# Recalibrating a build-time scheduler: the table of instruction durations is set to the pitches and latencies of a trace

## The chip, the core and the metric

The kernel runs on one NeuronCore of a Trainium2 chip. The metric is the device time of one execution in microseconds (us); lower is better. The engines are named as in the profile: PE (TensorE, matmuls; PEld is its weight load), ACT (ScalarE), DVE (VectorE), POOL (GpSimd), SP (SyncE, which issues the DMAs here).

## The reference

The kernel computes a transformer block with layer norms ahead of attention and of the feed-forward part, in bfloat16, for one sequence of 2048 tokens of width 1024, with 32 heads of 32 and a hidden width of 3584:

```python
def _A_ref(x, wqkv, wo):                       # attention
    qkv = (x @ wqkv).reshape(B, S, 3, H, Dh)   # H = 32, Dh = 32
    ...
    scores = jnp.einsum("bhqd,bhkd->bhqk", q, k) * scale
    p = _softmax(scores, axis=-1)
    o = jnp.einsum("bhqk,bhkd->bhqd", p, v)
    return o.transpose(...).reshape(B, S, D) @ wo

def _B_ref(x, w1, b1, w2, b2):                 # feed-forward
    h = _gelu(jnp.einsum("bsd,df->bsf", x, w1) + b1)   # tanh form
    return jnp.einsum("bsf,fd->bsd", h, w2) + b2

h  = x + _A_ref(_layernorm(x), A_wqkv, A_wo)
h2 = h + _B_ref(_layernorm(h), B_w1, B_b1, B_w2, B_b2)
```

## The kernel before

The program is a straight line of instructions for each engine, with no loop at run time. When it is built, Python code first describes the work as tasks in a graph (`Graph.add`): a task has an engine, one or several instructions, the buffers it reads and writes, a priority, an *occupancy* (`occ`, how long its engine is taken) and a *latency* (`lat`, how long after that its result can be used by another engine). `Graph.schedule` then plays the tasks through in time: whenever an engine is free by these figures, it takes one of the tasks whose inputs are ready by these figures. The order in which each engine takes its tasks in that play is the order in which its instructions are written into the program. `Graph.assign` adds the semaphore waits that the dependencies need. The figures themselves reach the chip in no other way: an instruction starts there when it is at the head of its engine's queue and its semaphores are there, whatever the plan thought.

The choice on ACT, DVE, POOL and SP is by priority and then by position in the list of tasks. PE has a rule of its own, `pick_pe`: a score matmul task (`qk`) goes first if it is ready; the value matmuls (`pv`) and the denominator matmuls (`den`) follow when enough rounds are waiting (`PV_FORCE = 3`, `PV_START = 6`); otherwise the next task of the background (`bg`) is taken, that is, projections, output projection, FFN and transposes. PE is in one of three tiling modes, `row` for qk (four matmuls of 32 rows at once), `col` for pv, den and narrow background (four of 32 columns at once), and `full`; a change of mode is charged `switch`. `merge_tiles` turns some runs of narrow background tasks back into full matmuls after the order is fixed.

The work is tiled as follows. There are 8 query blocks of 256 tokens (`qb`) and 8 head groups of 4 heads (`g`), so 64 attention jobs, each with 8 rounds (`r`) of 256 keys. One round is one qk task of eight matmuls (L769), two exponentials of 128x1024 from PSUM into SBUF on ACT (L779), a pv task of eight matmuls (L805), an addition of key halves on DVE (L820) and a denominator task against a matrix of ones (L834). Scores use PSUM banks 0 to 5 as three units of two banks, and a round takes two units, so that the qk of the next round needs the first exponential of this one to be done. Banks 6 and 7 are slots for attention results and for background.

In time there is a *lead* (x is loaded, normalised and transposed, keys and values of the first head group are projected half a chunk at a time, and two jobs of attention run beside it), then the other head groups and query blocks with the rest of the projections, late queries, the output projection (`wo`, evicted at L910), the second layer norm (`ln2`), `ffn1` (evicted at L943, with GELU by a tanh at L965 on ACT) and `ffn2` (evicted at L989) as background, and at the end the part of the last query block that needs the last attention results: `wo(7)`, `ln2(7)`, `ffn1(7)` (L540, GELU at L952) and `ffn2(7)`. Narrow background matmuls have line L534, their merged form L537, full ones L540; transposes by PE are L604, their evictions L611 and L613; L598 is the layer norm's scaling and L583 its statistics. Weights come through rings of buffers: 4 blocks of 512 KB for `wo` and `ffn1` (`a_w1r`) and 7 for `ffn2` (`a_w2r`).

Of the kernel before, what the change touches and what calls it, by code (L numbers as in the profile page):

```python
# [10 lines left out]
E = mybir.EngineType  # L11
# [49 lines left out]
class Graph:  # L61
# [44 lines left out]
        return t  # L106


    def schedule(self, pick_pe, pool, switch=0.1, dma_rate=280.0, dma_lat=2.1, dma_issue=0.06):
        for i, t in enumerate(self.tasks):  # L110
            t.left = len(t.deps)
            for d in t.deps:
# [8 lines left out]
        n = 0  # L121
# [207 lines left out]
def build_kernel(nc, A_x, A_wqkv, A_wo, B_w1, B_b1, B_w2, B_b2, out):  # L329
# [154 lines left out]
    B_qd = [[gr.buf() for _ in range(NCH)] for _ in range(G)]  # L484


    MM = 0.2195
    def c_dve_ps(n):
        return (120 + n) / 960.0 + 0.02

    def c_dve(n, x=1):
        return (62 + n / x) / 960.0 + 0.085

    def c_act(n, ap_bias=False):
        return 0.073 + (0.093 if ap_bias else 0.0) + n / 1200.0

    def pe(fns, occ, reads=(), writes=(), kind="bg", mode="full", prio=0, after=()):
        return gr.add(E.PE, fns, occ, 0.16, reads, writes, prio, kind, mode, after)

    def slot(nrel=1):  # L500
        return Slot(gr.buf(), nrel, (6, 7))
# [13 lines left out]
    def bb(bank):  # L515
        return bank.buf if isinstance(bank, Slot) else B_ps[bank]
# [10 lines left out]
    def mm(bank, lhsT, rhs, start, stop, reads, narrow, cols=(0, 512), after=()):  # L527

        c0, c1 = cols
        occ = MM * (c1 - c0) / 512.0 + 0.003  # L530
        if narrow:
            fns = []
            for j in range(4):
                fns.append(lambda p, j=j: p.matmul(psum[32 * j:32 * j + 32, bi(bank), c0:c1], lhsT[:, 32 * j:32 * j + 32], rhs,  # L534
                                                   start=start, stop=stop, tile_position=(0, 32 * j), skip_group_check=True))
            t = pe(fns, occ, reads=reads, writes=[bb(bank)], mode="col", after=after)
            t.whole = lambda p: p.matmul(psum[:, bi(bank), c0:c1], lhsT, rhs, start=start, stop=stop,  # L537
                                         skip_group_check=True)
        else:
            t = pe(lambda p: p.matmul(psum[:, bi(bank), c0:c1], lhsT, rhs, start=start, stop=stop),  # L540
                   occ, reads=reads, writes=[bb(bank)], mode="full", after=after)
        take(t, bank)

    def act(fn, n, reads=(), writes=(), prio=0, ap_bias=False, kind="", after=()):
        return gr.add(E.Activation, fn, c_act(n, ap_bias), 0.14, reads, writes, prio, kind, after=after)

    def dve(fn, occ, reads=(), writes=(), prio=0):
        return gr.add(E.DVE, fn, occ, 0.08, reads, writes, prio)

    def pool(fn, occ, reads=(), writes=(), prio=0):  # L550
        return gr.add(E.Pool, fn, occ, 0.1, reads, writes, prio)
# [22 lines left out]
    def layer_norm(tiles, prio, norm="dve", stats=None):  # L574

        n = len(tiles)
        while cnt["ln"] % NLN + n > NLN:
            cnt["ln"] += 1
        i = cnt["ln"] % NLN
        cnt["ln"] += n  # L580
        for k, (x_ap, B_x, o_ap, B_o) in enumerate(tiles):
            for c in range(2):
                dve(lambda v, c=c, k=k, x_ap=x_ap: v.bn_stats(st_l[:, i + k, 6 * c:6 * c + 6], x_ap[:, 512 * c:512 * c + 512]),  # L583
                    0.68, reads=B_x if isinstance(B_x, list) else [B_x], writes=[B_stl[i + k]], prio=(prio or 1) if stats is None else stats)
            dve(lambda v, k=k: v.bn_aggr(mv_l[:, i + k, :], st_l[:, i + k, :]), 0.2,  # L585
                reads=[B_stl[i + k]], writes=[B_mv[i + k]], prio=prio)
        sl = slice(i, i + n)
        pool(lambda g: g.tensor_copy(mvb[:, sl, :], mv_l[:, sl, :]), 0.25, reads=B_mv[sl], writes=B_mvb[sl], prio=prio)  # L588
        dve(lambda v: v.tensor_copy(mvr[:, sl, :], mvb[:, sl, 0:1]), 0.2, reads=B_mvb[sl], writes=B_mvr[sl], prio=prio)
        pool(lambda g: g.tensor_scalar(tb[:, sl, :], mvb[:, sl, 1:2], EPS_BF, None, ALU.add), 0.25,  # L590
             reads=B_mvb[sl], writes=B_tb[sl], prio=prio)
        pool(lambda g: g.tensor_tensor(denb[:, sl, 0], tb[:, sl, 0], cexp[:, 0:n], ALU.pow), 0.42 + 0.157 * n,
             reads=B_tb[sl] + [B_cexp], writes=B_denb[sl], prio=prio)
        pool(lambda g: g.tensor_tensor(rden[:, sl, 0], denb[:, sl, 0], cexp[:, 8:8 + n], ALU.pow), 0.4 + 0.157 * n,
             reads=B_denb[sl] + [B_cexp], writes=B_rden[sl], prio=prio)
        for k, (x_ap, B_x, o_ap, B_o) in enumerate(tiles):
            eng, cost = (dve, 0.58) if norm == "dve" else (pool, 3.8)
            eng(lambda e, k=k, x_ap=x_ap, o_ap=o_ap: e.tensor_scalar(  # L598
                o_ap, x_ap, mvr[:, i + k, :], rden[:, i + k, :], ALU.subtract, ALU.mult), cost,
                reads=(B_x if isinstance(B_x, list) else [B_x]) + [B_mvr[i + k], B_rden[i + k]], writes=[B_o], prio=prio)  # L600

    def transposes(src_ap, B_src, bank, dst_ap, B_dst, evac, prio):
        for dc in range(DC):
            t = pe(lambda p, dc=dc: p.transpose(psb[:, bi(bank), dc * P:(dc + 1) * P], src_ap[:, dc * P:(dc + 1) * P], ident[:]),  # L604
                   0.064, reads=[B_src, B_ident], writes=[bb(bank)], prio=prio)
            take(t, bank)

        def src():
            return psb[:, bi(bank), :].rearrange("p (dc t) -> p dc t", dc=DC)
        if evac == "act":  # L610
            t = act(lambda a: a.activation(dst_ap, src(), ACT.Copy), 1024, reads=[bb(bank)], writes=[B_dst], prio=-1)  # L611
        else:
            t = dve(lambda v: v.tensor_copy(dst_ap, src()), 0.70, reads=[bb(bank)], writes=[B_dst])  # L613
        drop(t, bank)


# [130 lines left out]
    class Att:  # L747
# [8 lines left out]
        def qk(self, job, r):  # L756


            qb, g = job
            qs = q_slots[qb, g]  # L760
            us = [self.unit % self.n_units, (self.unit + 1) % self.n_units]
            self.unit += 2
            fns, banks = [], []
            for i in range(2):
                for h in range(4):
                    k0 = (2 * r + i) * P

                    def fn(p, i=i, h=h, k0=k0):
                        return p.matmul(psum[:, 2 * us[h // 2] + h % 2, 256 * i:256 * i + 256],  # L769
                                        KT[32 * h:32 * h + 32, g, k0:k0 + P], QT[32 * h:32 * h + 32, qs, :],  # L770
                                        start=True, stop=True, tile_position=(32 * h, 0))
                    fns.append(fn)
            for u in us:
                banks += [B_ps[2 * u], B_ps[2 * u + 1]]
            pe(fns, 0.224, reads=[B_KT[8 * g + r], B_QT[qs]], writes=banks, kind="qk", mode="row")
            s = self.rounds % NR
            self.rounds += 1
            for k, u in enumerate(us):
                act(lambda a, u=u, k=k: a.activation(PT[:, s, k, :, :], psum[:, 2 * u:2 * u + 2, :], ACT.Exp, bias=0.0, scale=SCALE),  # L779
                    1024, reads=[B_ps[2 * u], B_ps[2 * u + 1]], writes=[B_PT[2 * s + k]], kind="exp")  # L780
            return s
# [7 lines left out]
    class Job:  # L789
# [8 lines left out]
        def pv(self, r, s):  # L798
# [8 lines left out]
                        PT[:, s, h // 2, h % 2, 256 * i:256 * i + 256], start=first and i == 0, stop=last and i == 1,  # L807
                        tile_position=(0, 32 * h), skip_group_check=True))
            rd = [B_PT[2 * s], B_PT[2 * s + 1], B_V[NT * g + 2 * r], B_V[NT * g + 2 * r + 1]]
            t = pe(fns, 0.224, reads=rd, writes=[self.B_O, self.B_D] if first else [self.B_O], kind="pv", mode="col")  # L810
            take(t, bank)
            while self.sums:
                self.den(*self.sums.pop(0), False)
# [14 lines left out]
        def den(self, n, direct, last):  # L828
            bank = self.bank
            fns = []  # L830
            for i in range(2 if direct else 1):
                for h in range(4):
# [1 line left out]
                    fns.append(lambda p, h=h, rhs=rhs, i=i: p.matmul(  # L834
                        psum[32 * h:32 * h + 32, bi(bank), 256:512], ones32[:, :], rhs,
                        start=False, stop=last, tile_position=(0, 32 * h), skip_group_check=True))
            t = pe(fns, 0.224 if direct else 0.112, reads=[B_PT[2 * n], B_PT[2 * n + 1]] if direct else [B_PS[n]],
                   writes=[self.B_D], kind="den", mode="col")
            if last:
                closing.add(t)  # L840
# [1 line left out]
        def finish(self):  # L842
# [4 lines left out]
            B_O, B_D = B_OD[o]  # L847
            final = qb == 2 * NCH - 1 and g == G - 1
            D = OD[:, o, 1, :].rearrange("p (b j) -> p b j", j=32)
            t = dve(lambda v: v.transpose(OD[:, o, 1, :], psum[:, bi(bank), 256:512]), 0.445,  # L850
                    reads=[self.B_O, self.B_D], writes=B_D, prio=-1)
            drop(t, bank)
            if final:
# [3 lines left out]
                t = dve(lambda v: v.tensor_copy(OD[:, o, 0, :], psum[:, bi(bank), 0:256]), c_dve_ps(256),  # L857
                        reads=[self.B_O, self.B_D], writes=B_O, prio=-1)
            drop(t, bank)
            dve(lambda v: v.reciprocal(rr[:, o, :], D[:, :, 0]), 0.185, reads=B_D, writes=[B_rr[o]], prio=0)  # L860
            dve(lambda v: v.transpose(D, rr[:, o, :].unsqueeze(2).to_broadcast([P, 8, 32])), c_dve(256),
                reads=[B_rr[o]], writes=B_D, prio=0)
            for k in range(2 if final else 1):
# [140 lines left out]
    for tt in range(4, 8):  # L1004
        x_tile(tt, -5)
    for k in range(80):
        pe(lambda p: p.matmul(psum[:, 6, 0:256], ident[:, :], b2t[:, 0:256], start=True, stop=True), 0.12,  # L1007
           reads=[B_ident, B_b2t], writes=[B_ps[6]], kind="warm")
    LEAD_LAG = 2
    lead_jobs = [Job(0, 0, 6), Job(1, 0, 5)]  # L1010
# [241 lines left out]
```

## Time and profile before

| what | value |
|---|---|
| device time, median of 3 runs | 1100.69 us (1100.36 to 1102.47) |
| profiled execution, span from first to last instruction | 1099.2 us |
| granted clock of TensorE, mean | 0.997 |
| ACT busy | 1019.8 us, 93% |
| PE busy | 1056.5 us, 96% (matmuls are pipelined, their ends are modelled) |
| DVE busy | 757.2 us, 69% |
| POOL busy | 47.8 us, 4% |
| bytes moved by DMA | 174.43 MB, mean 159 GB/s |

The profiled execution's own device time is not recorded apart from its span; the span is 1.5 us below the median of the runs. An engine's busy time counts an instruction from its start to its end as recorded. Neighbouring instructions of one engine overlap in these records, so the mean duration of a group is longer than the distance from one instruction to the next (the *pitch*). The idle time behind a group is put down to the engine that released the wait last.

### The profile page before, as it was taken

The page shows a single profiled execution, that of the slowest core. Times are in us where ns is not written, and L with a number is a line of the kernel's source. Part 1 is how long each engine was busy: PE and PEld are TensorE (multiplying, and loading weights), DVE is VectorE, ACT ScalarE, POOL GpSimd, SP SyncE. Part 2 cuts the span into 40 slices and gives each one's busy share as a digit, 9 for nine tenths or more (in the row PEclk, how much of TensorE's full clock was granted, in tenths as well). Part 3 has the DMA queues.
Part 4 walks back from the last instruction along what each step waited for, and adds up shares of the span by engine and source line. Part 5 has one row for each costly group of instructions (what it writes and reads, how often), then busy time and mean ns, then how long its engine had stood idle before and what let it go on. Part 6 is the DMA issues. An engine that isn't in the chain of part 4 may idle for free.

```text
span 1099.2 us, 42056 instructions
## 1 busy us (share of the span) xinstructions
PE 1056.5 (96%) x19177; PEld 613.8 (56%) x19226; DVE 757.2 (69%) x1444; ACT 1019.8 (93%) x1124; POOL 47.8 (4%) x110
## 2 busy tenths in 40 slices
PE   8899999998899999999999899999999999999998
PEld 6655555553345744664475456546744664565483
DVE  7746666665676886788588768876886787687501
ACT  3879999999999999999999999999999999999650
POOL 3200000000000001001000100010010000000100
PEclk9999999999899999999999999999999999999999
DMA  6820000048345654854576466448654747797370
GB/s 184 227 103 2 29 2 3 2 159 268 115 122 154 189 151 150 260 162 149 185 228 188 150 203 180 143 150 255 181 178 149 216 142 239 243 266 242 98 262 20
DMA packets 265506, 174.43 MB, mean 159 GB/s; under 512 B 26864, under 2 KB 260336, under 8 KB 264560
## 3 DMA queue, kind: packets, MB, share of 16 engines
q1 hardware_dynamic: 265328, 171.74, 51.2%
q8 instruction: 151, 2.47, 0.9%
q14 instruction: 27, 0.22, 0.1%
HBM read 161.23 MB, written 10.49 MB: 156 GB/s over the span
## 4 chain that ended last, share of the span: by engine, by line
ACT 79%; PE 19%; DVE 1%; issue 0%; DMA 0%; POOL 0%; POOLq 0%; DVEq 0%
ACT PT L779 75%; PE ps L540 6%; ACT uu L965 4%; PE ps L537 4%; PE ps L534 3%; PE ps L769 2%; PE ps L805 1%; PE ps L1007 1%; PE ps L834 1%; DMA a_w1r<-in_A_wo_dram 0%; ACT xnT L611 0%; PE ps L604 0%; DVE PS L820 0%; DVE OD L850 0%; DVE OD L857 0%
## 5 line engine op out<-in xcount | busy, mean ns | idle before, releaser
L779 ACT ACTIVATE PT<-ps 128x1024 bf16<-128x1024 f32 x1024 | 953.6, 1189 | 18.2 <-PE ps L769 18.0
L820 DVE TENSOR_TENSOR PS<-PT 128x1024 bf16<-128x1024 bf16 x434 | 287.5, 686 | 124.5 <-ACT PT L779 63.8
L769 PE MATMUL ps<-QT,KT 32*128 32x256 bf16 x4096 | 204.6, 273 | 13.5 <-ACT PT L779 10.2
L805 PE MATMUL ps<-PT,V 128*32 128x256 bf16 x4096 | 179.9, 273 | 1.5 <-ACT PT L779 1.1
L769 PEld LDWEIGHTS ps<-QT,KT 32*128 32x128 bf16 x4096 | 61.0, 92 | 174.1 <-ACT PT L779 165.3
L834 PE MATMUL ps<-PS,ones 128*32 128x256 bf16 x1736 | 121.7, 274 | 2.0 <-DVE PS L820 2.0
L805 PEld LDWEIGHTS ps<-PT,V 128*32 128x32 bf16 x4096 | 103.8, 97 | 30.0 <-issue 8.7
L537 PE MATMUL ps<-a_w2r,gT 128*128 128x512 bf16 x445 | 109.6, 380 | 4.9 <-issue 2.4
L537 PE MATMUL ps<-hnT,a_w1r 128*128 128x256 bf16 x903 | 111.2, 273 | 1.1 <-DVE rr L860 0.5
L534 PE MATMUL ps<-hnT,a_w1r 128*32 128x256 bf16 x2660 | 96.9, 274 | 2.4 <-DVE gT L943 1.2
L537 PEld LDWEIGHTS ps<-hnT,a_w1r 128*128 128x128 bf16 x903 | 82.7, 98 | 25.1 <-issue 14.8
L943 DVE TENSOR_TENSOR gT<-ps,b1f 128x512 bf16<-128x512 f32 x98 | 67.3, 687 | 27.7 <-PE ps L534 18.4
L534 PE MATMUL ps<-a_w2r,gT 128*32 128x512 bf16 x1140 | 81.6, 381 | 2.5 <-DVE OD L857 2.5
L534 PEld LDWEIGHTS ps<-hnT,a_w1r 128*32 128x32 bf16 x2660 | 66.2, 96 | 18.5 <-issue 14.0
L537 PEld LDWEIGHTS ps<-a_w2r,gT 128*128 128x128 bf16 x471 | 40.4, 98 | 55.3 <-issue 15.7
L989 DVE SCALAR_TENSOR_TENSOR hch<-ps,hch 128x512 bf16<-128x512 f32 x32 | 22.0, 689 | 64.0 <-PE ps L540 47.1
L834 PEld LDWEIGHTS ps<-PS,ones 128*32 128x32 bf16 x1736 | 45.9, 96 | 22.8 <-issue 8.7
L965 ACT ACTIVATE uu<-uu 128x1024 bf16<-128x1024 bf16 x49 | 58.0, 1206 | 0.0
L537 PE MATMUL ps<-xnT,Wall 128*128 128x512 bf16 (+1 forms) x213 | 47.7, 360 | 2.3 <-issue 1.1
L588 POOL CAST mvb<-mv 128x2 bf16<-128x2 f32 (+1 forms) x25 | 6.1, 242 | 990.0 <-DVE mv L585 987.2
L706 DVE CAST V<-ps 128x512 bf16<-128x512 f32 x32 | 22.1, 690 | 30.8 <-PE ps L537 15.8
L537 PE MATMUL ps<-Wall,xnT 128*128 128x256 bf16 x327 | 41.0, 273 | 0.0
(85 smaller groups left out, 1009.8 us busy)
## 6 DMA issues: line engine op xcount, KB each, us to landing
a_w2r<-in_B_w_dram SPq DMA_DIRECT2D x105, 512.0 KB, 5.6
a_w1r<-in_B_w_dram SPq DMA_DIRECT2D x98, 512.0 KB, 4.4
a_w1r<-in_A_wo_dram SPq DMA_DIRECT2D x32, 512.0 KB, 4.0
b_w1r<-in_B_w_dram SPq DMA_DIRECT2D x14, 512.0 KB, 5.8
a_w1r<-in_A_wqkv_dram SPq DMA_DIRECT2D x11, 512.0 KB, 4.3
xrb<-in_A_x_dram SPq DMA_DIRECT2D x16, 256.0 KB, 4.2
Wall<-in_A_wqkv_dram SPq DMA_DIRECT2D x16, 256.0 KB, 4.8
hch<-in_A_x_dram SPq DMA_DIRECT2D x16, 256.0 KB, 4.0
```

What stands on the lines that cost most here:

```text
L534: fns.append(lambda p, j=j: p.matmul(psum[32 * j:32 * j + 32, bi(bank), c0:c1], lhsT[:, 32 * j:32 * j + 32], rhs, start=start, stop=stop, ...
L537: t.whole = lambda p: p.matmul(psum[:, bi(bank), c0:c1], lhsT, rhs, start=start, stop=stop, skip_group_check=True)
L540: t = pe(lambda p: p.matmul(psum[:, bi(bank), c0:c1], lhsT, rhs, start=start, stop=stop), occ, reads=reads, writes=[bb(bank)], mode="full" ...
L706: t = dve(lambda v: v.tensor_copy(dst, psum[:, bi(bank), :].rearrange("p (t g c) -> p g t c", t=2, g=2)), c_dve_ps(512), reads=[bb(bank)], ...
L769: return p.matmul(psum[:, 2 * us[h // 2] + h % 2, 256 * i:256 * i + 256], KT[32 * h:32 * h + 32, g, k0:k0 + P], QT[32 * h:32 * h + 32, qs, :],
L779: act(lambda a, u=u, k=k: a.activation(PT[:, s, k, :, :], psum[:, 2 * u:2 * u + 2, :], ACT.Exp, bias=0.0, scale=SCALE), 1024, reads=[B_ps[ ...
L805: fns.append(lambda p, i=i, h=h: p.matmul(psum[32 * h:32 * h + 32, bi(bank), 0:256], V[:, g, 2 * r + i, 32 * h:32 * h + 32], PT[:, s, h // ...
L820: dve(lambda v: v.tensor_tensor(PS[:, n, :, :], pairs[:, :, 0:256], pairs[:, :, 256:512], ALU.add), c_dve(1024, 2), reads=[B_PT[2 * s], B_ ...
L834: fns.append(lambda p, h=h, rhs=rhs, i=i: p.matmul(psum[32 * h:32 * h + 32, bi(bank), 256:512], ones32[:, :], rhs, start=False, stop=last, ...
L943: t = dve(lambda v: v.tensor_tensor(g[:, fc:fc + 2, :], psum[:, bi(bank), :].rearrange("p (f c) -> p f c", f=2), b1f[:, fc:fc + 2].unsquee ...
L965: act(lambda a: a.activation(w, w, ACT.Tanh, bias=0.0, scale=KT2), 1024, reads=[B_uu[i]], writes=[B_uu[i]], prio=-1)
L989: drop(dve(lambda v, hs=hs, bank=bank, half=half: v.scalar_tensor_tensor(hch[:, hs, c], psum[:, bi(bank), :], half, hch[:, hs, c], ALU.mul ...
```

## The change

Only figures change, in the calls that build the graph. In the table, "old" and "new" are us; n is the number of elements per partition.

| task | old occupancy + latency | new occupancy + latency |
|---|---|---|
| matmul of 512 columns | 0.2225 + 0.16 | 0.21593 + 0.2 (0.225 if narrow, that is, a list of matmuls) |
| qk | 0.224 + 0.16 | 0.222 + 0.225 |
| pv / den | 0.224 / 0.112 + 0.16 | 0.22 / 0.11 + 0.225 |
| mode switch | 0.1 | 0.104 |
| ACT, n = 1024 | 0.9263 + 0.14 | 0.9173 + 0.16 |
| DVE from PSUM, n = 512 | 0.678 + 0.08 | 0.600 + 0.135 |
| DVE 2x, n = 1024 | 0.683 + 0.08 | 0.598 + 0.135 |

The remaining edits are of the same kind. The figures for POOL and for DMA (`dma_rate`, `dma_lat`, `dma_issue`) and the rules of `pick_pe` stay as they are.

```diff
-    def schedule(self, pick_pe, pool, switch=0.1, dma_rate=280.0, dma_lat=2.1, dma_issue=0.06):
+    def schedule(self, pick_pe, pool, switch=0.104, dma_rate=280.0, dma_lat=2.1, dma_issue=0.06):
...
-    MM = 0.2195
+    MM = 0.21333
     def c_dve_ps(n):
-        return (120 + n) / 960.0 + 0.02
+        return (120 + n) / 960.0 - 0.058
 
     def c_dve(n, x=1):
-        return (62 + n / x) / 960.0 + 0.085
+        return (62 + n / x) / 960.0
 
     def c_act(n, ap_bias=False):
-        return 0.073 + (0.093 if ap_bias else 0.0) + n / 1200.0
+        return (0.064 if n == 1024 else 0.073) + (0.093 if ap_bias else 0.0) + n / 1200.0
 
     def pe(fns, occ, reads=(), writes=(), kind="bg", mode="full", prio=0, after=()):
-        return gr.add(E.PE, fns, occ, 0.16, reads, writes, prio, kind, mode, after)
+        return gr.add(E.PE, fns, occ, 0.225 if isinstance(fns, list) and len(fns) > 1 else 0.2, reads, writes, prio, kind, mode, after)
...
-        occ = MM * (c1 - c0) / 512.0 + 0.003
+        occ = MM * (c1 - c0) / 512.0 + 0.0026
...
     def act(fn, n, reads=(), writes=(), prio=0, ap_bias=False, kind="", after=()):
-        return gr.add(E.Activation, fn, c_act(n, ap_bias), 0.14, reads, writes, prio, kind, after=after)
+        return gr.add(E.Activation, fn, c_act(n, ap_bias), 0.16, reads, writes, prio, kind, after=after)
 
     def dve(fn, occ, reads=(), writes=(), prio=0):
-        return gr.add(E.DVE, fn, occ, 0.08, reads, writes, prio)
+        return gr.add(E.DVE, fn, occ, 0.135, reads, writes, prio)
...
-                    0.68, reads=B_x if ...          # layer norm's statistics
+                    0.595, reads=B_x if ...
...
-            eng, cost = (dve, 0.58) if norm == "dve" else (pool, 3.8)     # layer norm's scaling
+            eng, cost = (dve, 0.334) if norm == "dve" else (pool, 3.8)
...
-                   0.064, reads=[B_src, B_ident], ...   # transpose by PE
+                   0.0565, reads=[B_src, B_ident], ...
...
-            t = dve(lambda v: v.tensor_copy(dst_ap, src()), 0.70, ...)    # its eviction
+            t = dve(lambda v: v.tensor_copy(dst_ap, src()), 0.615, ...)
...
-            pe(fns, 0.224, reads=[B_KT[8 * g + r], B_QT[qs]], writes=banks, kind="qk", mode="row")
+            pe(fns, 0.222, reads=[B_KT[8 * g + r], B_QT[qs]], writes=banks, kind="qk", mode="row")
...
-            t = pe(fns, 0.224, reads=rd, ..., kind="pv", mode="col")
+            t = pe(fns, 0.22, reads=rd, ..., kind="pv", mode="col")
...
-            t = pe(fns, 0.224 if direct else 0.112, ..., kind="den", mode="col")
+            t = pe(fns, 0.22 if direct else 0.11, ..., kind="den", mode="col")
...
-            t = dve(lambda v: v.transpose(OD[:, o, 1, :], psum[:, bi(bank), 256:512]), 0.445,
+            t = dve(lambda v: v.transpose(OD[:, o, 1, :], psum[:, bi(bank), 256:512]), 0.36,
...
-            dve(lambda v: v.reciprocal(rr[:, o, :], D[:, :, 0]), 0.185, reads=B_D, writes=[B_rr[o]], prio=0)
+            dve(lambda v: v.reciprocal(rr[:, o, :], D[:, :, 0]), 0.1, reads=B_D, writes=[B_rr[o]], prio=0)
...
-        pe(lambda p: p.matmul(psum[:, 6, 0:256], ident[:, :], b2t[:, 0:256], start=True, stop=True), 0.12,   # warm-up
+        pe(lambda p: p.matmul(psum[:, 6, 0:256], ident[:, :], b2t[:, 0:256], start=True, stop=True), 0.109,
```

## The prediction

> **What bounds the kernel now.** I read the page's busy times and chain first, then asked who ACT waits for, in two windows.
>
> ```profile
> PE 1056.5 (96%) x19177; PEld 613.8 (56%) x19226; DVE 757.2 (69%) x1444; ACT 1019.8 (93%) x1124; POOL 47.8 (4%) x110
> ACT 79%; PE 19%; DVE 1%; issue 0%; DMA 0%; POOL 0%; POOLq 0%; DVEq 0%
> L779 ACT ACTIVATE PT<-ps 128x1024 bf16<-128x1024 f32 x1024 | 953.6, 1189 | 18.2 <-PE ps L769 18.0
> ```
>
> Four fifths of the chain is ACT, nearly all of it the 1024 exponentials of L779. They stood idle for only 18.2 us, 18.0 of that behind the score matmuls (qk, L769). The waits of ACT say where. The first answer below is for 0 to 75 us, the second for 75 to 1031 us, which is where the last exponential ends.
>
> ```profile
> ACT PT L779 <- PE ps L769: 15.0, 12, 3.8
> ...
> ACT PT L779 <- PE ps L769: 3.1, 4, 0.9
> ```
>
> So there are three stages. In the lead (0 to 75) ACT and PE take turns, and 15.0 us are lost in 12 waits. In the middle 956 us ACT stops four times, 3.1 us in all (4.3 us by the ends of its instructions, small hesitations counted). After 1031 come 68 us of PE work that needs the last attention result. The middle is 87% of the span and stands 0.4% above what ACT's own work takes, so a new order can win little there.
>
> Next, the durations on the chip, to set both tables against. The chain gives the exponential, the timeline the matmuls:
>
> ```profile
> 508.23 55.00 ACT PT L779 x60
> ...
> 551.39 0.40 PE L769 MATMUL ps<-QT,KT 32*128 32x256 bf16 x8
> 551.72 0.40 PE L534 MATMUL ps<-hnT,a_w1r 128*32 128x256 bf16 x8
> ...
> 1047.25 24.62 PE L540 MATMUL ps<-hnT,b_w1r 128*128 128x256 bf16 x224
> ...
> 1083.99 0.69 DVE L989 SCALAR_TENSOR_TENSOR hch<-ps,hch 128x512 bf16<-128x512 f32 x1 [5.35 <-PE ps L540]
> 1090.03 0.69 DVE L989 SCALAR_TENSOR_TENSOR hch<-ps,hch 128x512 bf16<-128x512 f32 x1 [5.35 <-PE ps L540]
> ```
>
> Sixty exponentials in 55.00 us are 0.9167 each; the mean of 1189 ns in the page's group is not the pitch, since neighbours overlap. From a qk to the next column-tiled matmul are 0.33 us, its mode switch included. 224 matmuls of 256 columns take 24.62 us, 0.1099 each. Between two evictions 6.04 us apart lie 28 matmuls of 512 columns, 0.2157 each.
>
> **The change part by part.** No instruction is added or removed. ACT still executes 1024 exponentials and 49 tanh, PE the same matmuls, and the same bytes move. What changes is the order on each queue, and with it the waits. I therefore ask what margin each table leaves per attention round: one qk, two exponentials, one pv, mostly one denominator matmul, and background matmuls (projections, FFN).
>
> *ACT.* Two exponentials: old table 2 x (0.073 + 0.8533) = 1.853, new 2 x (0.064 + 0.8533) = 1.835, chip 1.833.
>
> *PE.* On the chip qk with both switches takes 0.33 + 0.10 (0.096 in the trace for entering the row mode), pv and denominator 0.33 (0.219 + 0.109 by their starts), which leaves 1.833 - 0.76 = 1.07 for background. Old table: background 0.2225 for 0.2157 each, +0.034; pv and denominator 0.224 + 0.112, +0.008; qk and switches 0.424, -0.002. It overcharges PE by 0.040 a round and ACT by 0.020. So on the chip PE gained some 0.02 us a round on ACT against the plan. New table: background +0.001 on 512 columns and -0.006 on 256 (0.1093 for 0.1099), about -0.002 over the mix; pv and denominator 0.330, +0.002; qk and switches 0.430, +0.004; ACT +0.001. Margin left: about 0.003. The change takes 0.018 us a round.
>
> *What that costs.* The planner fills PE with background up to the moment when it believes the next qk ready, so qk can start up to one background matmul late. The chain shows the short path from an exponential's end to the next one:
>
> ```profile
> 39.99 0.05 issue
> 40.04 0.43 PE ps L769 x8
> 40.47 0.02 issue
> 40.49 1.95 ACT PT L779 x2
> ```
>
> With PE waiting ready that is 0.50. The cushion is what an exponential spends queued inside ACT: alone its record is 1.02 long, the mean is 1.189, so 0.17 us on average. In the trace's starts, in 118 of the 493 rounds of the middle, qk follows at once (within 55 ns); there a PE that is ahead gives its lead up again. Between two such rounds, about four apart, the lost margin adds up to 0.02 to 0.07 us; I take 0.06. In the trace 61 of the late rounds have a cushion under 0.06 us, and what they lack sums to 2.5 us. So **+2.5**, with 0 below (the other rounds keep their cushion) and 493 x 0.018 = 8.9 above (no round catches up).
>
> [...]
>
> *Loads.* The planner's DMA figures stay: a 512 KB block is given 0.9 + 1.87 + 1.2 = 4.0 us, and the page has 4.0 to 5.8 to landing. Background that runs ahead relative to ACT meets its weights earlier. PE's queue is in order: a matmul that waits for weights holds the qk behind it, and ACT behind that. One of the four stops of the middle is this: the chain has it as
>
> ```profile
> 691.77 5.03 DMA a_w1r<-in_A_wo_dram
> ```
>
> followed by an ACT wait of 0.63. I take **+1.0** (two more such stops), from 0 to 3.1 (as much as all four stops cost now).
>
> *DVE.* Occupancy falls by 0.08 and latency rises by 0.055, so dependent work sees 0.73 where it saw 0.76. In the trace DVE's 2x additions follow each other at 0.60, as the new table says. DVE is 69% busy; its cover is its idle third, and I put it at nothing. The layer norm's scaling is now 0.334 where its ends are 0.41 to 0.46 apart, 32 times, at most 32 x 0.12 = 3.8 us of DVE, hidden likewise while DVE has room; without it the next transposes would come that much later, mostly as lost background.
>
> *Lead.* Here plan and chip are bound by PE and ACT in turns, with data still arriving. Its longest ACT wait is 3.8 us, before 71 us, where queries and keys of the next head group are projected. Other choices could close it or open another one: **0**, from -3.8 to +3.8.
>
> *Tail.* Four matmuls of the background are still left at 1039, and their eviction (L989, 0.60) stands ahead of the second layer norm's statistics. A planner that counts background 3% cheaper finishes it sooner: **-0.6**, or +0.9 if four more are left over.
>
> Sum on the profiled execution: 1099.2 + 2.5 + 1.0 + 0 - 0.6 = 1102.1. The median of the runs is 1100.69, 1.5 above that span; I carry the 1.5: 1103.6.
>
> **The rivals.**
>
> *The margin was never needed* (0.22). PE stays within ACT's cushion, the stops of the middle move but keep their sum. For it: 0.17 us of mean cushion against a shift of 0.06, and a new table that is right to 0.6%. Against: thousands of choices change, and the lead has 15 us of waits to reshuffle. Time: 1100.7, within 1.5. An order that hardly changes would give the same time, and belongs here.
>
> *The lead closes up* (0.26), the other side. The new table has the projections 3% cheaper and evictions from PSUM free 0.08 earlier, so the planner can place qk ahead of projections where it now places it behind. The place is the wait of 3.8 us before 71 us; the gain decides once it exceeds the 3.5 that the middle loses above. If it closes and the middle keeps its 3.1: 1100.7 - 3.8 - 0.6 = 1096.3. Against it: that qk needs projected queries that PE must compute anyway, and the chain there is PE work without a hole.
>
> *PE becomes the bound* (0.12). If the small disturbances of PE (matmuls that follow 1 to 10 ns late, instruction fetches such as the 1.2 us of "issue" at 48 us) are never made up, the whole 0.018 is lost each round: 1100.7 + 8.9 + 1.0 = 1110.6. For it: PE is busy for 924 of the middle's 956 us. Against: that busy time contains the drains around qk, and some background runs dry, which lets PE catch up.
>
> **How the numbers follow.** My forecast, a few us lost in the middle, has 0.40, and a range of its own from 1102 to 1107. About 0.2% (2.2 us) is what a measurement of this kernel can tell from no change: its three runs span 1100.36 to 1102.47. Slower is the forecast plus PE as bound, 0.52; same 0.22; faster 0.26. The range goes from 1097.0, most of the way to the closed lead, to 1111.0, which holds the PE-bound case; outside I leave orders that win in lead and middle at once, or that starve on loads throughout.
>
> **What would show it.** Right: the waits of ACT for qk between 75 and 1031 us grow from 3.1 to some 5 to 8, in more than four pieces; the exponential's mean falls below 1189 ns, since its cushion is smaller; ACT's last exponential ends 2 to 5 us later; the 68 us after it change by under 1. Wrong: the middle's waits stay near 3 and the time moves with the lead; or the mean stays at 1189; or the 68 us after the last exponential move by more than 2, since then leftover background and not the margin decides.

## The result and the profile after

The changed kernel is slower: 1105.11 us median against 1101.27 us (nine runs each), a ratio of 1.0034 with a 95% interval from 1.0024 to 1.0044. Its profiled execution is the slowest of its nine, with a span of 1105.7 us for the 1099.2 us of before, so the trace shows 6.5 us where the medians show 3.8.

The page of the changed kernel, its busy times, its chain and the group of the exponentials (after the bar: busy time, mean in ns, idle time before it and what ended that):

```profile
PE 1058.8 (96%) x19327; PEld 616.2 (56%) x19373; DVE 752.6 (68%) x1444; ACT 1023.0 (93%) x1124; POOL 46.3 (4%) x110
ACT 50%; PE 43%; DVE 5%; issue 1%; POOL 1%; POOLq 0%; DVEq 0%
L779 ACT ACTIVATE PT<-ps 128x1024 bf16<-128x1024 f32 x1024 | 952.2, 1074 | 21.5 <-PE ps L769 21.1
```

ACT's share of the chain fell from 79% to 50% and PE's rose from 19% to 43%: through much of the kernel PE now hands the time on. The mean record of an exponential fell from 1189 to 1074 ns. Alone it is 1023 ns long (the 16 records before and 27 after that follow 0.1 us or more of idle time are all 1023 or 1024), so what the mean has above that, the cushion, went from 166 to 51 ns.

The waits of ACT, from 0 to 75 us and from 75 us to the last exponential (total, number, longest):

```profile
ACT PT L779 <- PE ps L769: 12.7, 13, 4.0
...
ACT PT L779 <- PE ps L769: 8.4, 12, 1.6
```

They fell by 2.3 us in the lead and rose from 3.1 to 8.4 in the middle. For exact sums I cut at two events that every kernel has, the ends of the 38th and of the last exponential. Idle in the middle is what the distances between ends of ACT's instructions exceed 0.9165 (exponential) or 0.935 (tanh); with 0.917 for the exponential, before has the 4.3 of the prediction in place of 4.8.

| us | before | after | difference |
|---|---|---|---|
| start to end of 38th exponential | 76.81 | 74.18 | -2.6 |
| from there to end of last exponential | 954.27 | 963.07 | +8.8 |
| (idle of ACT in it) | (4.8) | (13.6) | (+8.8) |
| last exponential to end | 68.07 | 68.44 | +0.4 |
| span | 1099.16 | 1105.69 | +6.5 |

How late qk comes is seen in the instructions' starts. The median distance from the end of the exponential that it needs to its start grew from 0.11 to 0.27 us, and the rounds in which it follows within 55 ns fell from 119 to 26 of 493.

Two more things show in the middle and at its end. One of the longest ACT waits, seen on PE in the timeline (in brackets, the idle time before and its releaser; "issue" means that the profile shows none):

```profile
449.13 0.73 PE L534 MATMUL ps<-hnT,a_w1r 128*32 128x256 bf16 x19 [0.84 <-issue]
```

Four such stops of PE, three of them inside a run of background and one before a denominator matmul (at 642.6 us), cost ACT 1.05, 1.17, 1.20 and 0.86 us. Before, the middle had one, which cost 1.00. And the clock, in windows of the changed kernel near the last exponential (1037 us):

```profile
1010.00:1016.00 6.00, 5.97 (x144) 2.87 (x132) 4.30 (x9) 5.98 (x8) 0.00 (x0) 1.00 0.57 167
1016.00:1022.00 6.00, 3.41 (x72) 1.12 (x64) 2.08 (x3) 6.00 (x8) 0.00 (x0) 0.99 0.16 44
1022.00:1039.00 17.00, 13.11 (x161) 4.22 (x162) 6.37 (x12) 14.91 (x17) 0.00 (x0) 0.50 0.17 50
```

The columns are length, busy time of PE, PEld, DVE, ACT and POOL, granted clock, DMA share and GB/s. At 1014 us the last background matmul that can run is done. From 1016 to 1022 us PE is busy for 3.4 of the 6 us, and then the clock is granted at 0.50 for 17 us, into the beginning of the tail. The chain has it there:

```profile
1036.42 0.63 PE ps L540
...
1037.39 1.78 PE ps L540 x4
```

Four matmuls of 512 columns in 1.78 us are 0.445 each, where 0.2157 was the pitch at a clock of 1.00 (28 of them in the 6.04 us up to 1090.03 us, before). Before, the clock was 1.00 from 284 us to the end of the work, and the background ended with the attention. (Both kernels have a shorter stage at 0.50 earlier, of 6.83 us, from 277.6 us before and from 274.4 us after. ACT loses 1.8 us between 270 and 300 us in both, so it is no part of the difference.) All nine runs of the changed kernel had a mean clock of 0.986 to 0.991.

### The profile page after: what moved, and what is told of

Its sections match the earlier page's. It is cut to its first block, busy times and chain, and to the rows that moved or that the text cites. A ratio compares the mean times of both kernels' runs of the same rounds, so it can differ in the third digit from the quotient of the medians.

```text
span 1105.7 us, 42340 instructions
## 1 busy us (share of the span) xinstructions
PE 1058.8 (96%) x19327; PEld 616.2 (56%) x19373; DVE 752.6 (68%) x1444; ACT 1023.0 (93%) x1124; POOL 46.3 (4%) x110
## 4 chain that ended last, share of the span: by engine, by line
ACT 50%; PE 43%; DVE 5%; issue 1%; POOL 1%; POOLq 0%; DVEq 0%
ACT PT L779 48%; PE ps L537 13%; PE ps L534 10%; PE ps L769 6%; PE ps L540 6%; PE ps L805 4%; PE ps L834 2%; ACT uu L965 2%; DVE PS L820 1%; PE ps L1007 1%; PE ps L604 1%; DVE gT L943 0%; DVE hch L910 0%; DVE uu L964 0%; DVE st L583 0%
## 5 line engine op out<-in xcount | busy, mean ns | idle before, releaser
L779 ACT ACTIVATE PT<-ps 128x1024 bf16<-128x1024 f32 x1024 | 952.2, 1074 | 21.5 <-PE ps L769 21.1
L805 PE MATMUL ps<-PT,V 128*32 128x256 bf16 x4096 | 182.2, 276 | 4.1 <-ACT PT L779 3.9
L537 PE MATMUL ps<-hnT,a_w1r 128*128 128x256 bf16 x927 | 113.5, 273 | 0.7 <-DVE rr L860 0.3
L534 PE MATMUL ps<-a_w2r,gT 128*32 128x512 bf16 x1436 | 103.9, 381 | 0.8 <-DVE gT L967 0.3
L537 PEld LDWEIGHTS ps<-hnT,a_w1r 128*128 128x128 bf16 x927 | 85.1, 98 | 24.9 <-issue 14.1
L534 PE MATMUL ps<-hnT,a_w1r 128*32 128x256 bf16 x2564 | 93.2, 274 | 5.1 <-issue 2.8
L537 PE MATMUL ps<-a_w2r,gT 128*128 128x512 bf16 x372 | 91.1, 380 | 5.6 <-issue 2.4
L534 PEld LDWEIGHTS ps<-hnT,a_w1r 128*32 128x32 bf16 x2564 | 63.2, 96 | 22.1 <-issue 18.3
L537 PEld LDWEIGHTS ps<-a_w2r,gT 128*128 128x128 bf16 x397 | 34.0, 98 | 47.1 <-issue 12.2
L965 ACT ACTIVATE uu<-uu 128x1024 bf16<-128x1024 bf16 x49 | 53.6, 1106 | 0.0
L537 PE MATMUL ps<-xnT,Wall 128*128 128x512 bf16 (+1 forms) x207 | 46.2, 360 | 1.7 <-issue 0.8
L534 PEld LDWEIGHTS ps<-a_w2r,gT 128*32 128x32 bf16 x1436 | 31.9, 96 | 27.2 <-issue 15.9
```

The lines of the kernel that those rows point to most:

```text
L805: fns.append(lambda p, i=i, h=h: p.matmul(psum[32 * h:32 * h + 32, bi(bank), 0:256], V[:, g, 2 * r + i, 32 * h:32 * h + 32], PT[:, s, h // ...
L965: act(lambda a: a.activation(w, w, ACT.Tanh, bias=0.0, scale=KT2), 1024, reads=[B_uu[i]], writes=[B_uu[i]], prio=-1)
```

## Experiments

The theory: what the figures overcharge is margin. Charged as long as they are, PE's tasks leave PE no lead on the plan, qk comes later, ACT's cushion goes and its idle time grows. The rival: any new order costs or wins a few us by chance. Each ratio below is against runs of the kernel before on the same chip. The columns "mean" (ns, exponential), "idle" (ACT in the middle), "stops" (of PE, over 0.45 us, in the middle, without a releaser and before a matmul that has no semaphore to wait for), "less stops" (the idle time without what these stops cost ACT) and "rest" (after the last exponential) are from the profiled execution.

| kernel | mean | idle | stops | less stops | rest | ratio, 95% interval |
|---|---|---|---|---|---|---|
| e2: old, PE's occupancies new | 1062 | 18.9 | 3 | 15.1 | 68.6 | 1.0124 (1.0106 to 1.0142) |
| e8: new, latencies old | 1064 | 18.6 | 2 | 16.4 | 68.6 | 1.0109 (1.0094 to 1.0125) |
| e4: new, again | 1070 | 13.2 | 2 | 10.8 | 68.3 | 1.0031 (1.0018 to 1.0043) |
| after (new) | 1074 | 13.6 | 4 | 9.3 | 68.4 | 1.0034 (1.0024 to 1.0044) |
| e6: new, filler matmuls | 1079 | 10.8 | 2 | 9.3 | 67.5 | 1.0017 (1.0006 to 1.0028) |
| e5: new, PE halfway | 1167 | 8.4 | 4 | 5.3 | 68.2 | 1.0020 (1.0007 to 1.0032) |
| e7: old, ACT and DVE new | 1184 | 9.9 | 4 | 4.9 | 69.4 | 1.0004 (0.9989 to 1.0018) |
| before | 1189 | 4.8 | 1 | 3.8 | 68.1 | 1 |
| e9: old, latencies new | 1189 | 8.4 | 4 | 5.5 | 79.8 | 1.0125 (1.0100 to 1.0150) |
| e10: e1, merged runs | 1203 | 3.6 | 2 | 2.2 | 67.1 | 0.9958 (0.9939 to 0.9978) |
| e11: e1, 32 more warm-up matmuls | 1206 | 6.3 | 3 | 2.8 | 67.1 | 0.9982 (0.9969 to 0.9995) |
| e3: old, ACT's occupancy new | 1211 | 3.7 | 3 | 1.9 | 79.9 | 1.0047 (1.0032 to 1.0063) |
| e1: new, PE's occupancies old | 1215 | 5.4 | 3 | 2.2 | 67.1 | 0.9954 (0.9936 to 0.9971) |
| e12: new, PE 3% above the old | 1245 | 3.5 | 4 | 1.8 | 91.3 | 1.0128 (1.0111 to 1.0145) |

The column "less stops" says more than "idle": over all fourteen profiles the idle time that is left falls from 15 to 16 us at a mean of 1062 to 1064 ns, over 9 to 11 at 1070 to 1079 and 4 to 6 at 1167 to 1189, to 2 to 3 from 1203 ns on. That is what the margin theory says of the cushion, for both tables, and chance of the order would not give it. It tells of the middle alone: the time depends on lead and rest too.

**PE's occupancies undone, and done alone.** In e1 the new table keeps PE's old occupancies:

```diff
-    MM = 0.21333
+    MM = 0.2195
-        occ = MM * (c1 - c0) / 512.0 + 0.0026
+        occ = MM * (c1 - c0) / 512.0 + 0.003
...   # qk 0.222 -> 0.224, pv 0.22 -> 0.224, den 0.11 -> 0.112, transpose 0.0565 -> 0.064, warm-up 0.109 -> 0.12
```

> The new table, with PE's occupancies alone set back to the old ones (latencies, DVE, ACT and the switch stay new). Margin theory: PE is overcharged by 0.046 a round and ACT by 0.001, so PE gains about 0.045 us a round on the plan. The exponentials' mean goes back to 1150 ns or more (1074 in the changed kernel, 1189 before), the idle time of the middle falls from 13.6 to 3 to 6 us, the background lasts to the end, so the granted clock goes back to 0.997, and the time is 1099 to 1102.5. Rival (it is the reshuffled order, the lead or the latencies, and not the margin): mean and idle time stay as in the changed kernel and the time is 1103 to 1107.

Measured: 1097.77 us, ratio 0.9954, faster than both and below the 1099 to 1102.5 expected. Mean and idle are as the margin theory had them, and the clock is 1.000. Margin alone explains the distance to the changed kernel and not the whole gain on the kernel before: e1's profile is 1.9 us shorter than before's, 1.5 of it in the lead and 1.0 in the rest, while its middle is 0.6 longer (three stops, 3.2 us, for one of 1.0; 1.6 shorter without them). In e2 the same lines go the other way, into the old table:

> The old table, with PE's occupancies alone set to the new ones (latencies, DVE, ACT and the switch stay old). Margin theory: PE is charged right to within 0.004 a round, ACT is overcharged by 0.020, so PE falls behind the plan by some 0.02 us a round, a worse margin than the changed kernel's 0.003. The exponentials' mean stays at or below 1080 ns, the idle time of the middle is 13 to 24 us, and the time 1105 to 1115, above the changed kernel. Rival (each reordering costs or wins a few us by chance): 1099 to 1105, with no relation to the mean of the exponentials.

Measured: 1116.15 us, slower than the changed kernel by 0.9%, as the margin theory had it, though 1.2 us above its range. The rival's times, up to 1105, are ruled out. The groups of the exponentials in e1 and e2:

```profile
L779 ACT ACTIVATE PT<-ps 128x1024 bf16<-128x1024 f32 x1024 | 954.6, 1215 | 18.5 <-PE ps L769 18.1
```

```profile
L779 ACT ACTIVATE PT<-ps 128x1024 bf16<-128x1024 f32 x1024 | 956.8, 1062 | 25.0 <-PE ps L769 23.9
```

The same edit moves mean and time the same way in both tables. In e1, 196 of 493 rounds have qk within 55 ns, against 26 in the changed kernel.

**The dose.** e5 sets PE's occupancies halfway (0.2192 for 512 columns), e12 above the old ones (0.229):

> The new table, with PE's occupancies halfway between the new ones and the old ones (0.2192 for a matmul of 512 columns, where the new table has 0.2159 and the old 0.2225). Margin theory as a dose: about 0.025 us a round, between the changed kernel (0.003) and the new table with old PE figures (0.045). The exponentials' mean lies between 1074 and 1215 ns, near 1160; the idle time of the middle is 5 to 9 us; the background runs dry a few us before the last exponential or not at all; time 1097 to 1102. Rival (chance of the order): no order between the three; anything from 1096 to 1108.

> The new table with PE's occupancies 3% above the old ones (0.229 for a matmul of 512 columns): the other end of the dose. The plan believes PE slower, so less background fits between two qk: the exponentials' mean is 1200 ns or more, the middle loses 2 to 5 us, but background is left behind the last exponential, whose 67 us grow to 75 to 95; time 1103 to 1125. Rival (more margin is better all the way): 1094 to 1099.

e5 came out between in mean and idle as expected, but at 1104.47 us (ratio 1.0020), above the 1097 to 1102 I had given; four stops of PE, costing ACT 3.1 us, are part of its 8.4. By its ratio it lies between the two, much nearer to the changed kernel. e12 has the longest mean and the least idle of all, and is slow at 1117.36 us, because 91.3 us come after its last exponential. Its chain there:

```profile
1025.26 3.67 PE ps L537 x32
1028.93 0.86 PE ps L540 x4
...
1030.06 10.82 PE ps L537 x49
```

This is background (L537) that the plan found no room for beside the exponentials. So the dose has two sides: too little margin costs idle time in the middle, too much leaves work behind it.

**ACT's figure alone, then DVE's with it.** e3 puts one edit into the old table, e7 that edit and DVE's occupancies and latency:

```diff
-        return 0.073 + (0.093 if ap_bias else 0.0) + n / 1200.0
+        return (0.064 if n == 1024 else 0.073) + (0.093 if ap_bias else 0.0) + n / 1200.0
```

> The old table, with the exponential's occupancy alone set to the new one (0.9173 for 0.9263). Margin theory: the overcharge of PE stays at 0.040 a round, that of ACT falls to 0.001, so PE gains 0.04 us a round, twice as much as before. The exponentials' mean is 1189 ns or more, the idle time of the middle 3 to 5 us, the clock 0.997, the time 1097 to 1102. Rival (an exact figure for the engine that bounds the kernel makes the plan tight, whichever engine it is): slower than before, 1102 to 1106.

> The old table with ACT's occupancy and all of DVE's figures (occupancy and latency) set to the new ones; PE's occupancies and latency, ACT's latency and the switch stay old. Beside it stands the run with ACT's occupancy alone, which left 12 us of background behind the last exponential. If it is DVE's long occupancy that slows the plan's background there (a bank is free later), the 80 us after the last exponential go back to 67 to 70, and the time is 1096 to 1100, as with the new table and old PE figures. If it is PE's and ACT's latency or the switch, 76 to 81 us stay behind the last exponential and the time is 1104 to 1108. Exponentials' mean above 1180 ns in both.

In e3 mean, idle and clock are as the margin theory had them, but the time, 1107.78 us, is not: I had forgotten the other side. The shorter exponential leaves the plan less PE time a round, and the background falls behind. Its last exponential ends at 1026.05 us, 5 us earlier than before, and the rest takes 79.9. In the chain of e3, from just after that end:

```profile
1026.95 1.19 PE ps L540 x5
...
1028.19 6.86 PE ps L537 x31
1035.04 1.96 PE ps L540 x9
```

e7 brings the rest back to 69.4, so it takes DVE's old figures to hold the background up; ACT's short figure and PE's overcharge alone do not (e1 has both, with a rest of 67.1). e7 sets DVE's occupancies and latency together. As the latency grew, the shorter occupancies, by which a bank comes free earlier in the plan, are the likely cause; no run separates the two. Its time, 1103.41 us, is above the 1096 to 1100 expected: its middle has four stops of PE that cost ACT 4.9 us, one of them 2.1.

**The latencies, undone and alone.** e8 sets 0.225 and 0.2, 0.16 and 0.135 back to 0.16, 0.14 and 0.08 in the new table; e9 puts the new ones alone into the old table:

> The new table with the three latencies (PE 0.16, ACT 0.14, DVE 0.08) set back to the old ones; all occupancies and the switch stay new. Margin theory: occupancies decide, the margin is 0.003 a round as in the changed kernel, the exponentials' mean stays below 1110 ns, the idle time of the middle is 9 to 16 us, the time 1102 to 1108. Rival (the long latencies make the plan start qk late): mean above 1130 ns, middle below 8 us, time below 1102.

> The old table with the three latencies alone set to the new ones (PE 0.2 or 0.225, ACT 0.16, DVE 0.135); all occupancies and the switch stay old. Corrected theory (too short a latency lets the plan count on results that are late on the chip, so long latencies are margin like long occupancies): cushion at or above that of before, mean 1189 ns or more, the idle time of the middle 3 to 6 us, and the background slower in the plan, so that some is left and the time behind the last exponential is 68 us or more; time 1099 to 1106. Rival (the latencies only help together with the short occupancies, the plan with both long is thrown off otherwise): mean below 1150 ns and the middle above 8 us.

e8 took 1114.53 us. Mean and a lost cushion were right, the size was not: it is 0.8% slower than the changed kernel (ratios 1.0109 and 1.0034), where I expected no difference to it. The long latencies are margin too: the changed kernel lost it with the occupancies and got part of it back with the latencies. The mean hardly shows this (1064 against 1074 ns); the idle time without stops does (16.4 against 9.3 us). e9, which has both long, has before's mean, idle time above the 3 to 6 expected (2.9 of its 8.4 are four stops), and 79.8 us after the last exponential, like e3. It took 1115.93 us, where I expected at most 1106. Either half of the change alone costs over 1%; together they cost 0.3%.

**The half clock.** e6 is the changed kernel with matmuls that nobody uses, taken only when PE has nothing else:

```diff
     ffn2(6, 0)
+    for k in range(51):
+        fs = slot()
+        ft = pe(lambda p, fs=fs: p.matmul(psum[:, bi(fs), :], ident[:, :], b2t[:, 0:512], start=True, stop=True), 0.216,
+                reads=[B_ident, B_b2t], writes=[bb(fs)], kind="warm", after=biased[6:7])
+        take(ft, fs)
+        drop(ft, fs)
     wo(7, True)
```

> The changed kernel with 51 matmuls of 512 columns added whose results nobody uses, chosen only when PE has nothing else, and only after FFN 1 of the last but one block: they fill the time in which the background has run dry. Until then the order is the changed kernel's. Theory that PE's idling halves the clock and that this costs time: no half clock near 1022 us, granted clock near 0.994 or above, the 68.4 us after the last exponential fall to 66 to 67.5, the middle loses 0.3 to 0.8 less, time 1.5 to 2.5 us below the changed kernel. Rival (the half clock only comes with the idling and costs nothing): clock up, time within 1 us of the changed kernel or, since the fillers delay qk, above it.

The same window as above, in e6:

```profile
1022.00:1039.00 17.00, 17.00 (x201) 7.40 (x200) 6.38 (x13) 13.29 (x17) 0.00 (x0) 1.00 0.12 33
```

The half clock is gone (mean 0.997), the rest fell by 0.9 us to 67.5, and with the added work the ratio is 1.0017, against 1.0034 and 1.0031 without. That is 1.5 to 1.9 us less, within what I expected, though the intervals overlap, so the gain in time is likely and not shown. Of the middle's 2.8 us between the two profiles nothing speaks for the clock: it is the cost of stops (1.5 us for 4.3).

**The changed kernel again, and the stops of PE.** e4 repeats it; e10 merges more narrow runs in e1 (`>= 3.0` becomes `>= 1.0` in `merge_tiles`); e11 makes 112 warm-up matmuls of e1's 80.

> The changed kernel once more, for a second profile of it beside the other runs. The stops of about 1 us in the middle at 450, 462, 643 and 865 us have no releaser in the profile. If they belong to the order of the instructions, they come at the same places again; if they are chance, they come elsewhere or in another number, and the span moves with them by 1 us each. The half clock from 1022 to 1039 us comes again in either case, since it follows PE's idling. Time 1104 to 1106, clock 0.986 to 0.991.

> The new table with PE's old occupancies, and runs of narrow background matmuls merged into full ones from 1.0 us of length on instead of 3.0: some 690 fewer matmuls, 1400 fewer instructions, 21 more mode switches. The stops of PE without a releaser come in all kernels at the same phase of the instruction stream (193 or 194 modulo 256) and 1.3 to 1.5 us after a 16 KB packet of instructions has landed. If they come from the supply of instructions, fewer and less dense instructions make fewer of them: 0 to 3 where the unmerged kernel had 4, and 0 to 2 us less. If the merging costs more switches than it saves, the time rises by 21 x 0.1 = 2 us at most. Time 1095 to 1100.

> The new table with PE's old occupancies, and 32 warm-up matmuls more (112 for 80), which PE takes in idle time before 40 us. All later instructions of PE stand 64 places later in its stream. If the stops without a releaser follow the packets of 256 instructions, they come at other places of the work than 459.5, 855.0 and 981.4 us, again at phase 193 or 194; if they follow the work (DMA traffic, the order), they come within a few us of the same places, at another phase. Time within 3 us of the unshifted kernel: 1095 to 1101.

e4 took 1105.95 us, again with half the clock, from 1022.15 us on. Of the four stops, those at 450 and 643 us came back at their places; the other two did not. e6, whose order is the changed kernel's until its filler begins, has the same two and no other (448.5 and 641.4 us). So of the four places of this order PE stopped at two in all three profiles, and at the other two in one. e10 has two stops for four (the lead's included) and a time equal to e1's within the intervals; it shows no gain beyond e1's. In e11 the stops, at 463.8, 558.5 and 862.3 us, stood again at phase 193 or 194 of the stream, 64 instructions earlier in the work. Two of the three lie within 8 us of places of e1, the lead of e11 being 3.4 us longer (most of the 4.3 us between the two profiles). The stops kept their phase of the stream; for the places the run is no proof.

## Why the prediction was right or wrong

Direction and time were right (1103.6 forecast, 1105.11 measured, 2.9 us forecast above before and 3.8 measured), by a sum whose terms were off against each other. That the number came so near is in part luck: between the two profiles the sum forecast 2.9 us and 6.5 were measured, and the medians lie closer together than the profiles.

*The margin of PE and the cushion of ACT* were the cause, as e1, e2, e5 and the mean show. The term was mis-sized: +2.5 us was forecast for the middle, with 8.9 as the upper end, and the middle lost 8.8 in the profiled run and 8.4 in e4. The step that failed was "between two such rounds, about four apart, the lost margin adds up". I took the number of rounds in which PE catches up for fixed. It fell from 119 to 26, so qk came 0.16 us later in the median, not 0.06. The prediction's own sum over the trace of before, taken with a shift of 0.10 us in place of 0.06, gives 6 us, and with 0.15 it gives 13. Three us of the 8.8 are more stops of PE, 4.3 us in place of 1.0; in e4, with two, they were 2.4. Without the stops the middle lost 5.5 us, and 7.0 in e4.

*Latencies.* I argued DVE's shift at nothing and left those of PE and ACT out of the margin. e8 prices all three at 0.8% in the new table.

*Loads* (+1.0): none of the four longest stops of the middle was a wait for weights; all four were PE's stops without a releaser. In the middle the waits of PE's weight loads for DMA were 1.5 us in three pieces before and 1.0 in two after, so the term came out at nothing; a loss of its size occurred, with a cause that the sum did not have.

*Lead* (0, from -3.8 to +3.8): -2.6, inside. The same order gave -1.9 in e4 and -3.0 in e6.

*Tail* (-0.6): +0.4. The background did end sooner, as the step said, but then PE idled and its clock was granted at 0.50 for 17 us, which I had not thought of. e6 shows about 0.9 us of it in the rest.

*The rivals.* The lead did win, as the second rival had it, but less than the middle lost. PE did become the bound in much of the middle, as the third rival had it. The truth lies between forecast and third rival. That exact figures would do no harm, the first rival, is refuted by e1 and e2.

*What would show it.* The waits of the middle came out at 8.4 us in 12 pieces (5 to 8 in more than four were forecast), the mean fell, the rest moved by under 1. The last exponential ended 6.2 us later, more than the 2 to 5 said.

## What to carry to other kernels

In a plan that is made at build time and played by in-order queues, exact figures need not be the best. What takes longer on the chip than in the plan delays whoever stands behind it (behind PE's stop of 0.84 us at 449 us in the changed kernel ACT stood for 0.94), and a task charged too long leaves time unused (with PE 6% too long, 91.3 us came after the last exponential, for 68.1 before). With the other figures new, PE charged exactly gave 1.0034 of before, 3% too long 0.9954, and 6% too long 1.0128; no run here charged PE's occupancies too short. So charge the engine that feeds the bottleneck a little too much, and check two numbers after each change: the cushion of the bottleneck (its mean record against its record alone) and how much background is left when it ends. A table may be wrong in several entries that cancel, so try a correction entry by entry before judging it as a whole; here one part of it undone gave the fastest kernel, 0.9954 of before.

## What the runs showed of the hardware

*PE's stops without a releaser stand at one phase of its instruction stream.* The stream is counted with two instructions for each weight load (the load and its matmul) and with PE's semaphore instructions. Of the 50 stops over 0.45 us in the fourteen profiles, the lead's included, 49 are at position 193 or 194 modulo 256, and 1.25 to 1.6 us after a 16 KB packet of the instruction queue had landed. The fiftieth, of 0.50 us in e7, is at 82 and stands before a matmul that has a semaphore to wait for. Those in the middle cost ACT up to 2.1 us each. Counted like this, the stream has 38,636 places before and 38,927 after, and the queue moved 151 and 152 packets: one for about 256 places, which agrees with the spacing of the stops. The 1.21 us of "issue" at 48.04 us of before, which the prediction names, is one of these stops: a packet had landed at 47.76 us, and PE went on at 49.25. Why one boundary stops and another doesn't stays open: 34 of the 49 follow a block of 256 that PE went through in 3.6 to 4.1 us, but some 240 other blocks that fast had none.

*The clock was halved where PE had little work.* In the changed kernel it fell to 0.50 at 1021.9 us, 8 us after the last background matmul and about 6 us after PE began to pause, and stayed there for 17.07 us; with e6's filler in the pauses it did not fall. The earlier stage is alike: before, PE was busy for 4.19 us from 274 to 281 us and the clock fell at 277.6; in e1, with 5.96 us there, it did not (mean clock 1.000). In the trace of the changed kernel the two stages at 0.50 are 6.83 and 17.07 us long, and the stage at 1.00 behind the second, which runs past the last instruction, 68.27: lengths as 2 to 5 to 20. What sets them is not shown. PE was not wholly idle before the fall at 1021.9 us: it was busy for 3.41 of the 6 us, with the qk, pv and denominator matmuls of every round, and the longest pause was 0.48 us. Which share of busy time keeps the clock up is not shown.
